# Decode attention with an MLP on one core: the output projection's weight moved behind the last V, read in contiguous rows and five pieces; the last V in wide form; o moved to the weight's layout by a matmul

## The chip, the cores and the metric

One core of a Trainium2 chip. The time is the device time of one execution in microseconds (us). Each kernel was executed several times; the text gives the median and the range. Profiles are single executions; their span, from the first to the last instruction, is 1.5 to 1.9 us shorter than the device time of the same execution. "Head n" counts from 0; the last head is 31. The granted clock is the share of its full clock that the profile records as given to TensorE. A transfer *lands* when its last completion signal arrives, and only then do the engines that wait for it go on. SBUF is the on-chip memory for operands, PSUM the one that TensorE writes its results to.

## The reference, cut to what matters

```python
# x: 1 x 640.  32 heads, 32768 cached keys, head size 128, all bf16.
xn = layernorm(x)
q = (xn @ wq) as 32 heads of 128
scores = q . k_cache[h] / sqrt(128);  p = softmax(scores);  o[h] = p @ v_cache[h]
out = x + concat(o) @ wo + (silu(xn @ w_gate) * (xn @ w_up)) @ w_down      # wo: 4096 x 640
```

K and V are 32 x 8.39 MB each and are read once: 537 of the 554 MB that the kernel moves. `wo`, the weight of the output projection, has 5.24 MB.

## The kernel before

Everything big passes through three slots of 64 KB per partition in SBUF (`ring`). SyncE issues all loads in one queue, in the order of `units`: wq, the MLP's weights, then K of head h and V of head h-1 in turn, then `wo`, then the last V in five pieces. A load waits until the slot's last reader is done.

```python
    TAIL = [128, 64, 32, 16, 16]          # the last V's pieces, in key blocks of 128 keys
    W = 512 // DH                         # 4
    ...
    units += [("wo",), ("v", H - 1)]
    ...
    # wo: partition = position within a head, so 32 rows of 1280 B for each partition
    e.dma_start(wo, A_wo.rearrange("(h d) n -> d h n", d=DH)).then_inc(s_wo, 16)
```

There are two forms of P·V. In the *wide* form (all heads but the last) four columns of P are the stationary operand and four V blocks stream past as 512 columns. The result lies in four partitions and must be copied out (`evac`), added up across partitions by eight small matmuls (`fold`) and written to the o column (`column`). In the *narrow* form (last head) one V block of 128 x 128 is the stationary operand and one column of P streams past; 256 such matmuls leave o as a finished column.

```python
    def pv_half(h, half):                                           # wide: 64 matmuls for a head
        for j in range(half * NJ // 2, (half + 1) * NJ // 2, W):
            mm = t.matmul(O, lhsT=P[:, h % PR, j:j + W], rhs=ring[:, s, j * DH:(j + W) * DH], ...)
    ...
    def pv_last():                                                  # narrow: 256 matmuls
        for i, n in enumerate(TAIL):
            t.wait_ge(s_tail[i], 16)
            for _ in range(n):
                mm = t.matmul(OL, lhsT=ring[:, s, j * DH:(j + 1) * DH], rhs=P[:, h % PR, j:j + 1], ...)
                j += 1
    ...
    def att(h):                                                     # projection: 5 matmuls for a head
        for c in range(NCD):
            mm = t.matmul(acc[:, c:c + 1], lhsT=wo_v[:, h, :, c], rhs=ocol[:, h:h + 1], ...)
        return mm
    ...
    # the end of TensorE's program (heads 2 to 31 are a loop of three heads a turn)
    fold(H - 2)
    t.wait_ge(s_wo, 16)
    for h in range(H - 1): att(h)         # 31 heads, 155 matmuls, while the last V lands
    total(H - 1)
    pv_last()
    t.wait_ge(s_ov, H)
    att(H - 1).then_inc(s_att, 1)         # 5 matmuls; then VectorE adds x, and the output is stored
```

## Time and profile before

| | before |
|---|---|
| time, median of 4 runs (range) | 1294.53 us (1294.24 to 1294.67) |
| span of the profiled run | 1292.7 us |
| bytes moved, mean rate over the span | 554 MB, 429 GB/s |
| last K lands / V of head 30 lands | 1234.5 / 1253.9 us |
| `wo` lands / last V's last piece lands | 1268.3 / 1287.8 us |
| granted TensorE clock, mean | 0.884 |

From the page of before: the span, and the busy share of the DMA engines in tenths and the GB/s that they moved, in 40 equal slices of the span.

```profile
span 1292.7 us, 9645 instructions
...
DMA  9999999999999999999999999999999999999997
GB/s 400 449 424 427 443 426 437 432 436 434 432 434 436 426 436 436 430 432 438 432 436 430 436 434 430 434 436 428 434 438 432 430 438 436 432 430 436 436 392 311
```

Read it as: the kernel is one stream of bytes, full from the start to the last slice. The chain of waits of before, its end (start in us, length, what):

```profile
1262.78 25.06 DMA ring<-in_A_v_cache_dram
...
1287.88 0.60 PE ps L279 x16
...
1288.51 0.23 DVE ocol L505
...
1288.79 0.37 PE ps L345 x5
...
1289.19 0.16 DVE outb L508
```

The last V piece lands at 1262.78 + 25.06 = 1287.84 us. Then come 16 narrow matmuls, a scaling on VectorE, 5 projection matmuls, the final addition, and the store. TensorE's part of the timeline of before (start, length, engine, line, operation, output<-inputs, shapes, count, and in brackets the idle time in front and what ended it):

```profile
1262.87 7.07 PE L266 MATMUL ps<-ring,P 128*4 128x512 bf16 x32
...
1273.40 6.33 PE L345 MATMUL ps<-ocol,ring 128*128 128x1 bf16 x155 [0.35 <-ACT ocol L391]
...
1280.02 1.76 PE L279 MATMUL ps<-P,ring 128*128 128x1 bf16 x61
1282.06 3.55 PE L279 MATMUL ps<-P,ring 128*128 128x1 bf16 x128 [0.27 <-issue]
1285.80 1.50 PE L279 MATMUL ps<-P,ring 128*128 128x1 bf16 x51 [0.19 <-issue]
1287.88 0.59 PE L279 MATMUL ps<-P,ring 128*128 128x1 bf16 x16 [0.59 <-DMA ring<-in_A_v_cache_dram]
1288.79 0.36 PE L345 MATMUL ps<-ocol,ring 128*128 128x1 bf16 x5 [0.32 <-DVE ocol L505]
```

L266 is wide P·V: 32 matmuls in 7.07 us, 221 ns each. L345 is the projection: 40 ns each. L279 is narrow P·V: 27 ns each, so 256 take about 7 us where the wide form takes 14.1 us. TensorE has hardly an idle moment between 1273.4 and 1287.3 us and then waits 0.59 us for the last piece. DMA and TensorE are nearly level at the end, and the 155 projection matmuls sit where the last V is still landing. Busy time by stretch, with the granted clock (PEclk), the DMA's busy share and GB/s:

```profile
core 0: us, PE busy (x) PEld busy (x) DVE busy (x) ACT busy (x) POOL busy (x), PEclk, DMA share, GB/s
...
1255.00:1261.00 6.00, 6.00 (x31) 2.49 (x28) 1.15 (x3) 0.00 (x0) 0.00 (x0) 1.00 1.07 363
...
1276.00:1280.00 4.00, 4.00 (x96) 4.00 (x95) 0.00 (x0) 0.00 (x0) 0.00 (x0) 0.50 0.98 414
...
1284.00:1288.00 4.00, 3.22 (x116) 3.08 (x114) 0.00 (x0) 0.00 (x0) 0.00 (x0) 0.50 0.20 77
```

Two things to see. In the stretch that carries `wo` (1255 to 1261) the DMA engines are fully busy but move 363 GB/s, not the 430 of the slices before. And from 1273.9 us on the granted clock is 0.50, although TensorE is busy all the time: with one-column matmuls.

### The profile page before, as it was taken

What the parts mean: (1) busy time and instruction counts of PE and PEld (TensorE: products, weight loads), DVE (VectorE), ACT (ScalarE), POOL (GpSimd) and SP (SyncE); (2) the same over time, 40 slices, a digit from 0 to 9 for tenths busy, and PEclk for the clock granted to TensorE, in tenths of its full rate; (3) what the DMA queues carried; (4) which work ended last, traced back from release to release, by engine and by line L of the source; (5) the groups of instructions that cost most, each with busy time, mean ns of one, the idle gap of its engine ahead of it and who ended that gap; (6) DMA issues with size and microseconds to landing.
All of it is one profiled execution on the core that took longest, in us unless ns stands there. A gap on an engine that the chain in (4) does not pass through costs nothing.

```text
span 1292.7 us, 9645 instructions
## 1 busy us (share of the span) xinstructions
PE 1040.2 (80%) x5147; PEld 264.2 (20%) x3227; DVE 669.9 (52%) x407; ACT 50.8 (4%) x139; POOL 1.1 (0%) x8
## 2 busy tenths in 40 slices
PE   4688879877779877779877779877778877779878
PEld 1301222111222111222111222111222111222116
DVE  0485544666444666444666444666444666444660
ACT  2000000000000000000000000000000000000000
POOL 0000000000000000000000000000000000000000
PEclk9588899888899888889888889888899888899887
DMA  9999999999999999999999999999999999999997
GB/s 400 449 424 427 443 426 437 432 436 434 432 434 436 426 436 436 430 432 438 432 436 430 436 434 430 434 436 428 434 438 432 430 438 436 432 430 436 436 392 311
DMA packets 14721, 554.20 MB, mean 429 GB/s; under 512 B 1329, under 2 KB 5490, under 8 KB 5746
## 3 DMA queue, kind: packets, MB, share of 16 engines
q1 hardware_dynamic: 14704, 554.00, 99.4%
q8 instruction: 9, 0.15, 0.0%
q14 instruction: 6, 0.05, 0.0%
q10 hardware_dynamic: 2, 0.00, 0.0%
HBM read 553.99 MB, written 0.00 MB: 429 GB/s over the span
## 4 chain that ended last, share of the span: by engine, by line
DMA 54%; PE 30%; DVE 13%; issue 2%; SPq 1%; DVEq 0%
DMA ring<-in_A_k_cache_dram 52%; PE ps L266 16%; DVE ring L479 13%; PE ps L227 12%; DMA ring<-in_A_v_cache_dram 2%; PE ps L254 1%; SPq L174 1%; PE ps L303 0%; PE ps L297 0%; SPq L183 0%; DVE sc L485 0%; PE ps L279 0%; SPq L185 0%; DVE pmax L491 0%; SPq L182 0%
## 5 line engine op out<-in xcount | busy, mean ns | idle before, releaser
L479 DVE TENSOR_TENSOR ring<-ring,qb 128x8192 bf16<-128x8192 bf16 x128 | 557.8, 4421 | 88.4 <-DMA ring<-in_A_k_cache_dram 88.4
L227 PE MATMUL ps<-ring,ident 128*128 128x512 bf16 x1920 | 498.7, 418 | 0.0
L266 PE MATMUL ps<-ring,P 128*4 128x512 bf16 x1984 | 438.3, 379 | 0.0
L254 PE MATMUL ps<-ring,ident 128*128 128x512 bf16 x128 | 56.1, 439 | 224.2 <-DVE ring L479 223.6
L266 PEld LDWEIGHTS ps<-ring,P 128*4 128x4 bf16 x1984 | 166.0, 85 | 245.4
L254 PEld LDWEIGHTS ps<-ring,ident 128*128 128x128 bf16 x128 | 12.6, 99 | 622.2 <-DVE ring L479 350.4
L499 DVE TENSOR_SCALAR negb<-ps 128x1 f32<-128x1 f32 x32 | 5.1, 158 | 215.5 <-PE ps L309 215.5
L485 DVE TENSOR_REDUCE sc<-ps 128x64 f32<-128x512 f32 x128 | 82.3, 686 | 63.0 <-PE ps L227 63.0
L494 DVE TENSOR_REDUCE m<-ps 1x1 f32<-1x128 f32 x32 | 8.9, 278 | 192.2 <-PE ps L303 192.2
L403 ACT ACTIVATE P<-sc,negb 128x256 bf16<-128x256 f32 x32 | 16.2, 508 | 1185.1 <-DVE negb L499 1185.1
L297 PEld LDWEIGHTS ps<-rsum,ones 128*128 128x128 f32 x64 | 12.3, 194 | 99.1 <-issue 98.3
L289 PE MATMUL ps<-identf,o 4*128 4x1 f32 x248 | 31.8, 245 | 0.9 <-ACT o L386 0.9
L289 PEld LDWEIGHTS ps<-identf,o 4*128 4x128 f32 x248 | 30.0, 187 | 0.9 <-ACT o L386 0.9
L386 ACT ACTIVATE o<-ps,rzb 4x512 f32<-4x512 f32 x31 | 21.0, 677 | 0.0
L219 PE MATMUL ps<-ring 128*128 128x512 bf16 x40 | 11.3, 455 | 11.0 <-DMA ring<-in_A_wq_dram 11.0
L449 DVE TENSOR_SCALAR sg<-sg 128x13 f32<-128x13 f32 (+1 forms) x2 | 0.2, 156 | 34.2 <-ACT sg L379 34.2
L491 DVE TENSOR_REDUCE pmax<-sc 128x1 f32<-128x256 f32 x32 | 13.4, 420 | 0.0
L303 PE MATMUL ps<-identf,pmax 128*1 128x128 f32 x64 | 12.2, 273 | 1.2 <-DVE pmax L491 1.2
L330 PE MATMUL ps<-xn,ring 128*128 128x1 bf16 (+1 forms) x140 | 8.8, 199 | 4.6 <-DMA ring<-in_B_w_down_dram 4.6
L309 PE MATMUL ps<-m,ones 1*128 1x1 f32 x64 | 12.1, 256 | 0.4 <-DVE m L494 0.4
L309 PEld LDWEIGHTS ps<-m,ones 1*128 1x128 f32 x64 | 9.4, 182 | 14.2 <-issue 13.5
L468 DVE RECIPROCAL rzb<-ps 128x1 f32<-128x1 f32 x32 | 5.1, 158 | 9.8 <-PE ps L297 9.8
(50 smaller groups left out, 88.8 us busy)
## 6 DMA issues: line engine op xcount, KB each, us to landing
ring<-in_A_wq_dram SPq DMA_DIRECT2D x1, 5120.0 KB, 15.2
ring<-in_A_wo_dram SPq DMA_DIRECT2D x1, 5120.0 KB, 37.0
ring<-in_A_v_cache_dram SPq DMA_DIRECT2D x1, 4096.0 KB, 22.3
ring<-in_B_w_gate_dram SPq DMA_DIRECT2D x1, 2160.0 KB, 19.9
ring<-in_B_w_up_dram SPq DMA_DIRECT2D x1, 2160.0 KB, 24.6
ring<-in_B_w_down_dram SPq DMA_DIRECT2D x1, 2080.0 KB, 28.5
ring<-in_A_v_cache_dram SPq DMA_DIRECT2D x1, 2048.0 KB, 21.6
ring<-in_A_v_cache_dram SPq DMA_DIRECT2D x1, 1024.0 KB, 23.6
```

What stands on the lines that cost most here:

```text
L174: e.dma_start(ring[:, s, j * DH:(j + n) * DH], kv_src(A_v_cache, u[1], j, n)).then_inc(s_tail[i], 16)
L227: return t.add_instruction(mybir.InstMatmult(start_tensor_calc=False, stop_tensor_calc=stop, tile_size=(128, 128), tile_position=(0, 0), l ...
L254: t.matmul(ob, lhsT=ident[:, :], rhs=src, start=True, stop=False)
L266: mm = t.matmul(O, lhsT=P[:, h % PR, j:j + W], rhs=ring[:, s, j * DH:(j + W) * DH], start=(j == 0), stop=(j + W == NJ))
L289: mm = t.matmul(fold_ps, lhsT=o4[:, m * DH:(m + 1) * DH], rhs=identf[0:W, m:m + 1], start=(m == 0), stop=(m == W - 1))
L297: t.matmul(misc[:, 129:130], lhsT=ones[:, :], rhs=rsum[:, h % SR:h % SR + 1], start=True, stop=True).then_inc(s_z, 1)
L309: t.matmul(misc[:, 128:129], lhsT=ones[0:1, :], rhs=m1[0:1, h % SR:h % SR + 1], start=True, stop=True).then_inc(s_b, 1)
L386: a.activation(out=o4[:, :], in_=O, func=ACTF.Copy, scale=rzb[0:W, h % SR:h % SR + 1]).then_inc(s_o4, 1)
L403: a.activation(out=P[:, h % PR, :], in_=sc[:, :], func=ACTF.Exp, bias=negb[:, h % SR:h % SR + 1], scale=c_scale, accum_out=rsum[:, h % SR: ...
L479: v.tensor_tensor(out=kh, in0=kh, in1=q[:, None, :].to_broadcast([128, HF, DH]), op=ALU.mult).then_inc(s_mul, 1)
L485: v.tensor_reduce(out=sc[:, i * HF:(i + 1) * HF], in_=bank[i].rearrange("p (j e) -> p j e", e=G), axis=AX.X, op=ALU.add).then_inc(s_red, 1)
L491: v.tensor_reduce(out=pmax[:, h % SR:h % SR + 1], in_=sc[:, :], axis=AX.X, op=ALU.max).then_inc(s_max, 1)
```

## The change

The intent: read `wo` in long rows, which need a layout where partition p holds rows 32p to 32p+31; put it last, in pieces, so that the end of the stream is followed by only 10 projection matmuls; bring o into the same layout by one matmul. The last V takes the wide form, as the other heads have it. The diff, cut:

```diff
-    TAIL = [128, 64, 32, 16, 16]
+    TAIL = [128, 64, 32, 32]
+    RB = DH // 32; OC = H * DH // 128; WTAIL = [16, 8, 4, 2, 2]
-    units += [("wo",), ("v", H - 1)]
+    units += [("v", H - 1), ("wo",)]
...
-   e.dma_start(wo, A_wo.rearrange("(h d) n -> d h n", d=DH)).then_inc(s_wo, 16)
+   wo_src = A_wo.rearrange("(p j) n -> p (j n)", j=OC)
+   for i, n in enumerate(WTAIL):
+       e.dma_start(wo[:, j * D:(j + n) * D], wo_src[:, j * D:(j + n) * D]).then_inc(s_wo[i], 16)
+       j += n
...  pv_last:
+   t.wait_ge(s_o4, h)
-   for _ in range(n):
-       mm = t.matmul(OL, lhsT=ring[:, s, j * DH:(j + 1) * DH], rhs=P[:, h % PR, j:j + 1], ...)
-       j += 1
+   for _ in range(n // W):
+       mm = t.matmul(O, lhsT=P[:, h % PR, j:j + W], rhs=ring[:, s, j * DH:(j + W) * DH], ...)
+       j += W
...  the end of TensorE's program:
    fold(H - 2)
-   (wait for wo; att(0) to att(30))
    total(H - 1)
    pv_last()
-   t.wait_ge(s_ov, H); att(H - 1)
+   fold(H - 1)
+   t.wait_ge(s_ob, 1)
+   t.matmul(op, lhsT=oblk[:, :, :], rhs=fold32[:, :], start=True, stop=True)     # moves o
+   t.wait_ge(s_ot, 1)
+   for i, n in enumerate(WTAIL):
+       t.wait_ge(s_wo[i], 16)
+       (n x 5 projection matmuls: lhsT=wo_v[:, j, :, c], rhs=ot[:, j:j + 1])
...  ScalarE: evac(31), column(31), copy op -> ot;  VectorE: oblk = o columns x block pattern
```

Constants for the movement are made by GpSimd at the start.

More of the change, by code (lines that the diff above doesn't have):

```diff
@@ L46, in bass_parallel_sum__gqa_block_cached__swiglu_ffn__decode_kernel @@
     SR = 3
-    TAIL = [128, 64, 32, 16, 16]
+    TAIL = [128, 64, 32, 32]
+    RB = DH // 32
+    OC = H * DH // 128
+    WTAIL = [16, 8, 4, 2, 2]
     W = 512 // DH
-    assert sum(TAIL) == NJ and NHF == 4 and (H - H0) % PER == 0 and PER % SLOTS == 0
+    assert sum(TAIL) == NJ and all(n % W == 0 for n in TAIL) and NHF == 4 and (H - H0) % PER == 0 and PER % SLOTS == 0
     assert PER % PR == 0 and PER % SR == 0
+    assert OC == 32 and H * RB == 128 and sum(WTAIL) == OC
     c_scale = float(DH) ** -0.5
@@ L87, in bass_parallel_sum__gqa_block_cached__swiglu_ffn__decode_kernel @@
         ocol = sbt("ocol", [128, H], BF16)
+        oblk = sbt("oblk", [128, H, RB], BF16)
+        blk = sbt("blk", [128, RB], BF16)
+        fold32 = sbt("fold32", [128, OC], BF16)
+        ot = sbt("ot", [128, OC], BF16)
         hcol = sbt("hcol", [128, FB], BF16)
@@ L103, in bass_parallel_sum__gqa_block_cached__swiglu_ffn__decode_kernel @@
         s_slot = [sem(f"slot{i}") for i in range(SLOTS)]
-        s_x, s_wq, s_wo, s_out = sem("x"), sem("wq"), sem("wo"), sem("o")
+        s_x, s_wq, s_out = sem("x"), sem("wq"), sem("o")
+        s_wo = [sem(f"wo{i}") for i in range(len(WTAIL))]
         s_ffn = sem("ffn")
@@ L118, in bass_parallel_sum__gqa_block_cached__swiglu_ffn__decode_kernel @@
         s_att, s_fin = sem("att"), sem("fin")
+        s_ob, s_op, s_ot = sem("o_blocks"), sem("o_ps"), sem("o_rows")
         block = es.enter_context(nc.Block())
@@ L142, in hidden @@
             return w[:, c, FM * 128:F]
-        wo = flat[:, WO_S * CE:WO_S * CE + H * D].rearrange("p (h n) -> p h n", h=H)
-        wo_v = wo.rearrange("p h (m c) -> p h m c", c=NCD)
-        assert H * D <= CE
+        wo = flat[:, WO_S * CE:WO_S * CE + OC * D]
+        wo_v = wo.rearrange("p (j m c) -> p j m c", j=OC, c=NCD)
+        assert OC * D <= CE
         def kv_src(cache, h, j0, n):
@@ L152, in bass_parallel_sum__gqa_block_cached__swiglu_ffn__decode_kernel @@
             O = ps8[0:W, 4, :]
-            OL = ps8[:, 5, 0:1]
+            op = ps8[:, 5, 0:OC]
             acc = ps8[:, 6, 0:NCD]
@@ L187, in sp @@
                     else:
-                        e.dma_start(wo, A_wo.rearrange("(h d) n -> d h n", d=DH)).then_inc(s_wo, 16)
+                        wo_src = A_wo.rearrange("(p j) n -> p (j n)", j=OC)
+                        j = 0
+                        for i, n in enumerate(WTAIL):
+                            e.dma_start(wo[:, j * D:(j + n) * D], wo_src[:, j * D:(j + n) * D]).then_inc(s_wo[i], 16)
+                            j += n
                 e.wait_ge(s_fin, 1)
@@ L194, in pool, with done @@
             def pool(g):
-                for n, t in enumerate((ident, identf)):
-                    g.memset(t[:, :], 0.0).then_inc(s_const, 1)
-                    g.wait_ge(s_const, 2 * n + 1)
-                    g.affine_select(out=t[:, :], in_=t[:, :], compare_op=ALU.not_equal, fill=1.0, base=0,
-                                    pattern=[[-1, 128]], channel_multiplier=1).then_inc(s_const, 1)
+                n = [0]
+                def done(ins):
+                    ins.then_inc(s_const, 1)
+                    n[0] += 1
+                    g.wait_ge(s_const, n[0])
+                for t in (ident, identf):
+                    done(g.memset(t[:, :], 0.0))
+                    done(g.affine_select(out=t[:, :], in_=t[:, :], compare_op=ALU.not_equal, fill=1.0, base=0,
+                                         pattern=[[-1, 128]], channel_multiplier=1))
+                done(g.memset(blk[:, :], 0.0))
+                for a in range(RB):
+                    done(g.tensor_copy(out=fold32[a * 32:(a + 1) * 32, :],
+                                       in_=ident[a * 32:(a + 1) * 32, a * 32:a * 32 + OC]))
+                for a in range(RB):
+                    done(g.memset(blk[a * 32:(a + 1) * 32, a:a + 1], 1.0))
+                assert n[0] == 5 + 2 * RB
             @block.tensor
@@ L277, in pv_last @@
                         t.wait_ge(s_tail[i], 16)
-                        for _ in range(n):
-                            mm = t.matmul(OL, lhsT=ring[:, s, j * DH:(j + 1) * DH], rhs=P[:, h % PR, j:j + 1],
-                                          start=(j == 0), stop=(j == NJ - 1))
-                            j += 1
+                        for _ in range(n // W):
+                            mm = t.matmul(O, lhsT=P[:, h % PR, j:j + W], rhs=ring[:, s, j * DH:(j + W) * DH],
+                                          start=(j == 0), stop=(j + W == NJ))
+                            j += W
                     mm.then_inc(s_pv, 1)
@@ L341, in pe @@
                 mm.then_inc(s_fpd, 1)
-                def att(h):
-                    for c in range(NCD):
-                        mm = t.matmul(acc[:, c:c + 1], lhsT=wo_v[:, h, :, c], rhs=ocol[:, h:h + 1],
-                                      start=(h == 0 and c == 0), stop=(h == H - 1), skip_group_check=True)
-                    return mm
                 t.wait_ge(s_fx, 1)
@@ L357, in pe @@
                 fold(H - 2)
-                t.wait_ge(s_wo, 16)
-                t.wait_ge(s_ov, H - 1)
-                for h in range(H - 1):
-                    att(h)
                 total(H - 1)
                 pv_last()
-                t.wait_ge(s_ov, H)
-                att(H - 1).then_inc(s_att, 1)
+                fold(H - 1)
+                t.wait_ge(s_const, 5 + 2 * RB)
+                t.wait_ge(s_ob, 1)
+                t.matmul(op, lhsT=oblk[:, :, :], rhs=fold32[:, :], start=True, stop=True).then_inc(s_op, 1)
+                t.wait_ge(s_ot, 1)
+                j = 0
+                for i, n in enumerate(WTAIL):
+                    t.wait_ge(s_wo[i], 16)
+                    for _ in range(n):
+                        for c in range(NCD):
+                            mm = t.matmul(acc[:, c:c + 1], lhsT=wo_v[:, j, :, c], rhs=ot[:, j:j + 1],
+                                          start=(j == 0 and c == 0), stop=(j == OC - 1), skip_group_check=True)
+                        j += 1
+                mm.then_inc(s_att, 1)
             @block.scalar
@@ L408, in act @@
                 column(H - 2)
+                evac(H - 1)
+                column(H - 1)
+                a.wait_ge(s_op, 1)
+                a.activation(out=ot[:, :], in_=op, func=ACTF.Copy).then_inc(s_ot, 1)
             @block.vector
@@ L501, in dve @@
                 rz(H - 1)
-                h = H - 1
-                v.wait_ge(s_pv, H)
-                v.wait_ge(s_rz, H)
-                v.tensor_scalar(out=ocol[:, h:h + 1], in0=OL, scalar1=rzb[:, h % SR:h % SR + 1],
-                                scalar2=None, op0=ALU.mult).then_inc(s_ov, 1)
+                v.wait_ge(s_const, 5 + 2 * RB)
+                v.wait_ge(s_ov, H)
+                v.tensor_tensor(out=oblk[:, :, :], in0=ocol[:, :, None].to_broadcast([128, H, RB]),
+                                in1=blk[:, None, :].to_broadcast([128, H, RB]), op=ALU.mult).then_inc(s_ob, 1)
                 v.wait_ge(s_att, 1)
```

## The prediction

> **What bounds it now.** The page shows DMA busy in every slice, 429 GB/s over the span, and a chain of waits that is 54% DMA. That stream stays. The change touches the last 40 us, where the timeline and the table of windows say more than shares:
> - V of head 30 lands at 1253.8 us. From 1255.7 TensorE is busy nearly all the time: P·V of head 30 until 1269.9, its fold until 1273.05, 155 projection matmuls from 1273.4 (6.3 us, 40 ns each), 256 narrow P·V matmuls of the last head from 1279.8 (27 ns each, 7.1 us without waits), ending 1288.5. The last V piece lands at 1287.85: DMA is the limit by about half a microsecond only.
> - The span ends at 1292.7, 3.5 us after the last projection matmul.
>
> **What the change does.**
> 1. Weight rows of 1280 B become rows of 2.5 to 20 KB. In the windows that carry the weight (1254 to 1262) the DMA moves 363 GB/s at full busy share, against about 430 with V or K. Estimate: its 5.24 MB take 14.4 us now, 12.4 after. The Trainium skill, "DMA: Bandwidth & Descriptors", "Why small descriptors are slow", gives a fixed cost per packet; the trace agrees in direction. So the last byte lands about 2 us earlier, near 1285.8.
> 2. The last V in wide form: 64 matmuls of 512 columns. The loop's same form takes 7.07 us for 32 at full clock, so 14.1 us against 7.1. It cannot start before 1273.3: P of the last head exists at 1271.2 and fold(30) ends at 1273.05. V, moved ahead of the weight, is all there by about 1275, so this is TensorE time, not waiting.
> 3. Clock: TensorE does little between 1269.9 and 1273.3. The windows show the granted clock falling to 0.5 at 1273.9 in just this place; in earlier heads it comes back after a full busy window. The Trainium skill, "TensorE: Matmul & The Clock Gate", Part 1, has free-running windows of 3.4 us, and the clock record changes on that grid. So 3.4 to 6 us of the wide stage run at half clock: +1.7 to 3 us, my mean 1.9.
> 4. Then a new serial chain: evacuation 0.73, fold 1.08, column 0.2, block product about 0.3, movement matmul about 0.4, copy and hops about 0.4: 3.1 us.
> 5. Only then all 160 projection matmuls: 6.4 us, of which 155 stood earlier before and filled the time in which V was landing.
>
> **On the critical path.** TensorE becomes the limit by a wide margin: 1273.35 + 14.1 + 1.9 + 3.1 + 6.4 + 3.5 = 1302.4 us of span against 1292.7. The 2 us that DMA gains are not seen; the weight is complete before its matmuls begin. So +9.7 us: **1304.1 us**, 8 in 10 between 1301 and 1307. Chances: faster over 2% 0.01, within 2% 0.97, slower over 2% 0.02.
>
> **What would show it.** Everything up to 1270 unchanged; last weight piece landing near 1286; wide matmuls from about 1273.3 to 1289, part at half clock; no DMA wait in front of the projection matmuls, which run from about 1292.4 to 1298.8; the end of the chain of waits made of TensorE, with DMA idle for the last 13 us but for the output.
>
> **What would make it wrong.** If the clock does not fall (about 1302), or stays low over the wide stage (up to 1309). If projection matmuls run faster at full clock (up to 3 us less). If pieces came late enough for DMA to bound the end after all: about 1292 to 1294.

## The result, and the profile after

| | before | after |
|---|---|---|
| time, median (range), first 4 runs of each | 1294.53 (1294.24 to 1294.67) | 1304.58 (1302.02 to 1305.76) |
| ratio of the fast runs | | 1.0074, 95% interval 1.006 to 1.0089 |
| time, second set: 9 runs before, 5 runs after | 1294.21 (1293.92 to 1294.51) | 1303.80 (1303.37 to 1305.03) |
| ratio, second set | | 1.0076, interval 1.0062 to 1.009 |
| span of the profiled run | 1292.7 | 1302.0 |
| V of head 30 / last V / last of `wo` lands | 1253.9 / 1287.8 / 1268.3 | 1254.0 / 1273.6 / 1285.9 |
| spread of the runs, highest less lowest, first set | 0.43 | 3.74 |

The result is slower by 0.75% clear of noise.

From the page of after, the lines that answer to those of before:

```profile
span 1302.0 us, 9298 instructions
...
DMA  9999999999999999999999999999999999999994
GB/s 397 446 425 442 423 435 429 437 433 431 437 433 433 435 435 429 441 425 435 433 433 437 433 433 435 435 431 437 427 433 435 431 437 433 433 437 433 435 414 172
```

The last slice falls from 311 to 172 GB/s: the stream ends earlier, and the kernel later. The chain of waits of after, its end:

```profile
1272.17 1.05 PE ps L317 x8
1273.22 0.31 PE ps L325 x2
1273.54 15.61 PE ps L307 x64
...
1289.16 0.69 ACT o L417
...
1289.89 1.06 PE ps L317 x8
...
1290.98 0.18 ACT ocol L422
...
1291.26 0.30 DVE oblk L539
...
1291.69 0.19 PE ps L386
...
1291.91 0.21 ACT ot L443
...
1292.16 6.57 PE ps L393 x160
...
1298.76 0.16 DVE outb L542
```

No DMA stands in it after the last K, up to the final store. From 1273.5 us: wide P·V (L307), copy out, fold (L317), column, block product, movement matmul (L386), copy, and the 160 projection matmuls (L393). Busy time by stretch:

```profile
core 0: us, PE busy (x) PEld busy (x) DVE busy (x) ACT busy (x) POOL busy (x), PEclk, DMA share, GB/s
...
1272.00:1276.00 4.00, 3.83 (x17) 2.08 (x18) 0.17 (x1) 0.30 (x2) 0.00 (x0) 0.73 0.96 411
1276.00:1280.00 4.00, 4.00 (x17) 1.49 (x16) 0.00 (x0) 0.00 (x0) 0.00 (x0) 0.84 0.97 408
1280.00:1284.00 4.00, 4.00 (x21) 1.53 (x18) 0.00 (x0) 0.00 (x0) 0.00 (x0) 1.00 0.66 264
1284.00:1288.00 4.00, 4.00 (x20) 1.61 (x19) 0.00 (x0) 0.00 (x0) 0.00 (x0) 1.00 0.02 9
```

The clock drops to half at 1273.84 us and returns at 1277.25 us by the clock record, so 3.4 us of the wide stage ran at half speed. The stage took 15.66 us in place of 14.1. The DMA share is 0.02 from 1284 to 1288 us and 0.04 or less later, while the core computes for 13 us more.

Step by step, from the wide stage's start to the end of the span, in us:

| term | predicted | profiled run |
|---|---|---|
| wide stage starts | 1273.35 | 1273.46 |
| 64 wide matmuls at full clock + half clock | 14.1 + 1.9 | 15.66 in all |
| from their end to the first projection matmul | 3.1 | 3.0 |
| 160 projection matmuls | 6.4 | 6.57 |
| to the end of the span | 3.5 | 3.3 |
| last byte of `wo` lands | 1285.8 | 1285.9 |
| span | 1302.4 | 1302.0 |

### The profile page after: what moved, and what is told of

It is laid out like the page before. It is cut to its first block, busy times and chain, and to the rows that moved or that the text cites. A ratio compares the mean times of both kernels' runs of the same rounds, so it can differ in the third digit from the quotient of the medians.

```text
span 1302.0 us, 9298 instructions
## 1 busy us (share of the span) xinstructions
PE 1045.6 (80%) x4964; PEld 263.7 (20%) x3044; DVE 669.9 (51%) x407; ACT 51.9 (4%) x142; POOL 2.5 (0%) x17
## 4 chain that ended last, share of the span: by engine, by line
DMA 52%; PE 34%; DVE 12%; issue 2%; SPq 0%; ACT 0%; DVEq 0%
DMA ring<-in_A_k_cache_dram 52%; PE ps L293 17%; PE ps L254 13%; DVE ring L514 12%; PE ps L281 1%; PE ps L307 1%; PE ps L393 1%; PE ps L331 0%; PE ps L317 0%; PE ps L325 0%; ACT o L417 0%; SPq L193 0%; DVE sc L520 0%; PE ps L337 0%; SPq L195 0%
## 5 line engine op out<-in xcount | busy, mean ns | idle before, releaser
L293 PE MATMUL ps<-ring,P 128*4 128x512 bf16 x1984 | 438.3, 379 | 0.0
L317 PE MATMUL ps<-identf,o 4*128 4x1 f32 x256 | 32.9, 245 | 1.6 <-ACT o L417 1.6
L317 PEld LDWEIGHTS ps<-identf,o 4*128 4x128 f32 x256 | 31.0, 187 | 2.2 <-ACT o L417 2.2
L417 ACT ACTIVATE o<-ps,rzb 4x512 f32<-4x512 f32 x32 | 21.7, 678 | 15.7 <-PE ps L307 15.7
L307 PE MATMUL ps<-ring,P 128*4 128x512 bf16 x64 | 15.7, 411 | 0.0
```

Of the source, the lines that this page charges most:

```text
L317: mm = t.matmul(fold_ps, lhsT=o4[:, m * DH:(m + 1) * DH], rhs=identf[0:W, m:m + 1], start=(m == 0), stop=(m == W - 1))
L417: a.activation(out=o4[:, :], in_=O, func=ACTF.Copy, scale=rzb[0:W, h % SR:h % SR + 1]).then_inc(s_o4, 1)
```

## The experiments

Eleven kernels ran, all gave the right result. Each was timed in 5 rounds beside the kernel before on the same chip, so before has 9 runs in each of the three sets: medians 1294.21, 1294.27 and 1294.15 us. Line numbers differ between kernels by a few.

The theory, called A: after the last V the kernel is bound by TensorE's serial work, and the wide form is what makes it so. The rivals: the moved projection is the cost (B), the spread and the long wide stage are not the clock (C), the pieces matter. A further question, instruction fetch (D), came up on the way.

### Narrow last V in the changed kernel

```diff
 (after)  pv_last:
-   for _ in range(n // W): matmul(O, lhsT=P[.., j:j + W], rhs=ring[.. W blocks])
+   for _ in range(n): matmul(OL, lhsT=ring[.. block j], rhs=P[.., j:j + 1])
-   fold(H - 1);  evac(H - 1);  column(H - 1)
+   VectorE: ocol[:, 31] = OL * rz(31)
```

> The changed kernel with one part undone: the last V in narrow form again (256 matmuls of one column, output scaled straight into the o column; no evacuation, no fold). Weight still last, contiguous, five pieces, movement matmul kept. Theory A (the wide form is the cost, by TensorE time): narrow stage 1273.5 to 1280.4 us, block product, movement and copy until about 1281.7, 160 projection matmuls until 1288.2 with little or no wait for the weight pieces, span 1291.7, time about 1293.5 us, 1.0 us below the kernel before. Rival B (the order is the cost: 155 projection matmuls no longer fill the time in which V lands): about 6 us above the kernel before, 1299 to 1301 us, whatever the form.

Measured: 1295.21 us (1294.79 to 1295.46), ratio 1.0007 (0.9994 to 1.0021). TensorE's part of its timeline:

```profile
1273.56 5.92 PE L307 MATMUL ps<-P,ring 128*128 128x1 bf16 x217
1281.53 1.20 PE L307 MATMUL ps<-P,ring 128*128 128x1 bf16 x39 [2.04 <-issue]
...
1284.00 6.56 PE L392 MATMUL ps<-ot,ring 128*128 128x1 bf16 x160 [0.29 <-ACT ot L440]
```

Undoing the wide form alone takes back 8.6 of the 9.6 us (1303.80 to 1295.21). B expected 1299 to 1301 and falls: with the weight still last and all 160 projection matmuls behind the last V, the kernel is within 1.0 us of before. The 1.7 us over my expectation of 1293.5 come from a stop of 2.04 us after 217 of 256 matmuls, put down to "issue", that is, to nothing which the profile shows. It is taken up below. By the two profiles the 8.6 us are about these terms: 14.0 us of wide matmuls against 7.1 us of narrow ones, 1.7 us of half clock, 1.8 us more from the end of the stage to the first projection matmul (3.04 against 1.27 us, for evacuation and fold), less the 2.0 us of the stop.

### Wide last V in the kernel before

```diff
 (before)  pv_last: wide form as in the change;  then
+   fold(H - 1, into another bank);  evac(H - 1);  column(H - 1)
-   VectorE: ocol[:, 31] = OL * rz(31)
```

> The kernel before with one part of the change alone: the last V in wide form (evacuation, fold, column for head 31 as for the others), order and layout of the weight as before. Theory A: 155 projection matmuls until 1279.6 us as before, then 64 wide matmuls, the first 4 us of them at half clock, until about 1296, then evacuation, fold and column 2.1 us, 5 matmuls, span about 1302, time about 1304 us (9.5 us above before). Rival B: the wide matmuls hide behind the landing V, so only the last piece's 4 matmuls and the 2 us of evacuation show: 1295 to 1297 us.

Measured: 1304.06 us (1303.1 to 1304.24), ratio 1.0074 (1.006 to 1.0088). TensorE's timeline:

```profile
1273.70 6.33 PE L346 MATMUL ps<-ocol,ring 128*128 128x1 bf16 x155 [0.35 <-ACT ocol L393]
...
1280.39 16.25 PE L280 MATMUL ps<-ring,P 128*4 128x512 bf16 x64
...
1298.73 0.36 PE L346 MATMUL ps<-ocol,ring 128*128 128x1 bf16 x5 [0.27 <-ACT ocol L393]
```

The wide form alone costs 9.9 us here, without any of the other parts. The matmuls do not hide behind the landing V: the last piece is there at 1288.2 us, and the stage runs until 1296.6. It took 16.25 us, with the clock at half until 1285.0 us. With this run the four combinations are complete:

| last V | `wo` first, 1280 B rows | `wo` last, long rows, pieces, movement |
|---|---|---|
| narrow | 1294.2 | 1295.2 |
| wide | 1304.1 | 1303.8 |

The form decides, in either column; order and layout together move the time by 1 us or less.

### Keeping the clock up

```diff
 (after)
+   4 wide matmuls on old data, result thrown away
    fold(H - 2)
    total(H - 1)
+   4 more
    pv_last()
```

> The changed kernel with 8 wide matmuls on old data (result thrown away) put around the fold of head 30, where TensorE idles. Theory A says that the granted clock falls because that window has little wide work, and that this costs 1.7 to 3 us in the wide stage, varying with the phase of the clock's windows from run to run: here the clock should stay at 1.0, the wide stage take 14.1 us and start 0.9 us later, time about 1303.5 us with a spread under 1 us. Rival C (the spread over runs and the long wide stage have another cause, such as reads of V in competition with the landing weight): stage still 15.7 us, time about 1305.5 us, spread 2 to 4 us.

Measured: 1302.75 us (1302.65 to 1303.11), with 8 matmuls more than the changed kernel. Two rows of its busy time by stretch, and the wide stage in its timeline:

```profile
1272.00:1276.00 4.00, 4.00 (x24) 2.22 (x23) 0.17 (x1) 0.60 (x2) 0.00 (x0) 1.00 0.99 421
1276.00:1280.00 4.00, 4.00 (x20) 1.57 (x19) 0.00 (x0) 0.00 (x0) 0.00 (x0) 1.00 0.97 408
```

```profile
1274.66 13.98 PE L307 MATMUL ps<-ring,P 128*4 128x512 bf16 x64
```

The clock stays at 1.00 where it was 0.73 and 0.84. The stage starts 1.2 us later and takes 13.98 in place of 15.66 us. The spread over five runs is 0.46 us. So C falls: the fall of the clock is what lengthens the wide stage. The weight still landed during the stage here and did not lengthen it. That the fall comes at different moments in different runs, and so makes the spread of after, is a reading that fits and is not shown: the clock of the wide stage was seen in the profiled runs only, and the mean clock that each run lists (0.879 to 0.891 for the changed kernel) does not settle it. The nine times of the changed kernel lie within 0.4 us of 1302.0, 1303.7 or 1305.4 us, in steps of the 1.7 us that one such stretch at half clock costs.

### The changed kernel again

No edit; five more runs, with the profile.

> The changed kernel once more, for the spread over runs: both theories expect 1302 to 1306 us; theory A expects a wide stage of 14.1 us plus half of the time at half clock within it, whatever the profiled run shows.

Measured: 1303.80 us (1303.37 to 1305.03). The profiled run has the same wide stage, 15.66 us, of which 3.4 us at half clock by the clock record (1273.87 to 1277.29): 14.0 + 3.4 / 2 = 15.7. The range of the two sets together is 1302.02 to 1305.76 us.

### `wo` in one transfer, wide and narrow

```diff
-    WTAIL = [16, 8, 4, 2, 2]
+    WTAIL = [32]
```

> The changed kernel with the weight in one transfer in place of five. Theory A (TensorE time after the last V is the limit, the weight is there long before): no change, 1303 to 1305 us, with the transfer landed near 1286 us and the first projection matmul near 1292 us. Rival (the pieces are what makes the late weight bearable): 3 us or more slower than the changed kernel.

Measured on the changed kernel: 1303.59 us (1301.99 to 1303.74). The transfer landed at 1285.7 us; the first projection matmul started at 1292.2. Five pieces gain nothing there, because the weight is not what is waited for.

> The changed kernel with the narrow last V and the weight in one transfer. Here the projection was ready to start at 1284.0 us and the last byte came at 1285.8 us, so one transfer makes all 160 matmuls wait for it: start near 1286 us, about 2 us later than with five pieces, time about 1297.2 us against 1295.2 us. If pieces cost something of their own, the difference is smaller.

Measured with the narrow V: 1297.14 us (1297.05 to 1297.26), 1.9 us over five pieces.

```profile
1285.70 6.53 PE L392 MATMUL ps<-ot,ring 128*128 128x1 bf16 x160 [2.83 <-DMA ring<-in_A_wo_dram]
```

The projection was ready at about 1283.1 us (the copy of o had ended) and waited until the transfer landed at 1285.6. The stop after 217 narrow matmuls is here too, at 1.57 us. The pieces are worth something only after the wide form is gone.

### `wo` first in the queue, but contiguous

```diff
 (narrow V)
-    units += [("v", H - 1), ("wo",)];   TAIL = [128, 64, 32, 32]
+    units += [("wo",), ("v", H - 1)];   TAIL = [128, 64, 32, 16, 16]
```

> The changed kernel with the narrow last V and the weight ahead of it in the queue, as in the kernel before, but contiguous. Theory A: the transfer of the weight takes about 12.4 us in place of 14.4 us, the last V byte lands near 1285.8 us (1287.8 us before), but the o layout needs every head, so all 160 projection matmuls (6.5 us) stand after the last V: span about 1297.4 us, time about 1299 us. If the contiguous read itself gained nothing, the last V would land near 1287.8 us and the time be about 1301 us.

Measured: 1299.42 us (1299.14 to 1299.71). `wo` landed at 1266.2 us, 12.4 us after V of head 30 (1268.3 in before, 14.4 us after it), and the last V piece at 1285.8 (1287.8 in before). So the contiguous layout saves 2.0 us of DMA time. But in the new layout a column of o holds a part of every head, so no projection matmul can start before the last head is done: the first was at 1287.7 us, and 160 of them stood behind the last byte. In this layout the 2.0 us can be of use only with the order "weight last".

### The stop in the narrow stage: instruction fetch

In the narrow run the profile (its packed trace, packet by packet) has a packet of 16384 B in the queue that it calls "instruction", starting at 1279.0 us and taking 1.07 us; TensorE stopped from 1279.5 to 1281.5. The Trainium skill, "Runtime: NRT & Kernel Launch", "Instruction fetch mechanics", says that instructions are fetched in 16 KiB blocks of 256 (called pages below), the next while the current one runs. One narrow matmul is a weight load and a matmul, so 256 instructions are 128 pairs. If that is the cause, the stop belongs to a place in the instruction stream and must move when instructions are put in front.

```diff
 (narrow V)  at the start, where TensorE waits for data
+   for _ in range(90): matmul(unused column, lhsT=ident, rhs=ident[:, 0:1])
```

> The changed kernel with the narrow last V, and 90 matmuls of no use at the start of the kernel, where TensorE waits for data. In the run with the narrow last V, TensorE stood still for 2.04 us after 217 of 256 narrow matmuls, while a 16 KB packet of an instruction queue went over the DMA engines. Theory D (instruction fetch: the stream of short unrolled matmuls reaches a page of 256 instructions, or 128 load and matmul pairs, before it is there): the stop moves by 90 pairs to earlier places, after 127 and 255 matmuls, where the next one falls into the wait for VectorE and ScalarE; it shows less or not at all, time 1293.3 to 1294.3 us. Rival E (the stop belongs to the data, the landing of V or the weight): it stays after 217 matmuls, at 2 us, time 1295.2 us.

Measured: 1296.89 us (1296.59 to 1297.3). TensorE's timeline:

```profile
1273.30 3.47 PE L309 MATMUL ps<-P,ring 128*128 128x1 bf16 x127
1278.79 3.57 PE L309 MATMUL ps<-P,ring 128*128 128x1 bf16 x128 [2.02 <-issue]
1283.63 0.19 PE L309 MATMUL ps<-P,ring 128*128 128x1 bf16 x1 [1.27 <-issue]
```

The stops are after 127 and after 255 matmuls, as D says: 217 - 90 = 127, and one page further. E falls: the data came at the same times as in the run before (the last V at 1273.5 us in both). My time was wrong: I had expected the first stop to shrink in its new place, and it stayed at 2.02 us, with a second of 1.27 us behind it.

The kernel before has such stops as well, short ones: in its timeline above the idle times of 0.27 and 0.19 us put down to "issue" stand after 61 and after 189 narrow matmuls, 128 apart, and packets of 16384 B started at 1279.59 and 1283.46 us.

One estimate covers most of the stops. Taking a page to be entered 128 pairs before its end, at 25 to 27 ns a pair, the next page's first instruction ran 5.6 us after that entry in the narrow run (entered at about 1275.9 us, resumed at 1281.53) and 5.5 and 4.8 us in this one. A page of narrow pairs is used up in 3.2 to 3.4 us. It does not cover the second stop of before: that page was entered at 1282.06 us and the next one ran at 1285.80, 3.7 us later. What all eleven stops in the traces of this document share is the time from the start of the packet until TensorE goes on: 2.3 to 2.6 us. What varies is how long after the estimated entry the packet starts: 1.4 us at that stop, about 2.5 to 3.7 us at the others. Why it starts late is not shown, and that the fetch is asked for at the entry is inferred, not seen. The wide form never shows a stop: 128 wide pairs would last 28 us.

### Versions meant to beat both

```diff
 (narrow V)
-   fold(H - 2);  total(H - 1);  pv_last()
+   total(H - 1);  the first 128 narrow matmuls;  fold(H - 2);  the other 128
-   VectorE: ocol[:, 31] = OL * rz;  oblk = all columns x blk
+   VectorE, early: oblk of heads 0 to 30;  at the end: oblk[:, 31] = OL * rz * blk in one operation
```

> A version meant to beat both kernels: the changed kernel with the narrow last V, its first 128 matmuls put ahead of the fold of head 30 (TensorE idles there for 0.86 us), and the o block of the last head made in one VectorE operation straight from PSUM. By theory A and D: narrow stage from 1271.4 us, 7 us of matmuls, 1 us of fold and one stop of 1 to 2 us for an instruction page; block, movement and copy 0.9 us; projection from about 1282 to 1289 us; time about 1293.5 us (1292.5 to 1294), 0.7 us below the kernel before. If the stop does not depend on the instruction's place, or the earlier start runs into another wait, 1294.5 us or more.

Measured: 1293.19 us (1292.82 to 1293.31) against 1294.15 (1293.91 to 1294.39) before; ratio 0.9992, interval 0.9978 to 1.0005. TensorE's timeline:

```profile
1271.45 3.37 PE L309 MATMUL ps<-P,ring 128*128 128x1 bf16 x128
1274.76 1.86 PE L319 MATMUL ps<-identf,o 4*128 4x1 f32 x8
1276.55 2.53 PE L309 MATMUL ps<-P,ring 128*128 128x1 bf16 x89
1279.47 1.20 PE L309 MATMUL ps<-P,ring 128*128 128x1 bf16 x39 [0.40 <-issue]
...
1281.55 6.56 PE L393 MATMUL ps<-ot,ring 128*128 128x1 bf16 x160 [0.29 <-ACT ot L441]
```

Every run of it lies below every run of before, by 0.96 us in the median, but the interval does not exclude equal. It is 10.6 us under the changed kernel (1303.80). The stop after 217 matmuls has shrunk to 0.40 us: the fold in the middle, 1.9 us long, gives the fetch more time.

Then the last three heads were written out, so that the stream would run straight on and be fetched ahead:

```diff
-   with t.Fori(0, (H - H0) // PER) as i: ...
+   with t.Fori(0, (H - H0) // PER - 1) as i: ...
+   for h in range(H - PER, H): head(h)
```

> The same, with the last three heads taken out of TensorE's loop and written out, so that the instruction stream goes straight on through the slow wide matmuls of the last heads and pages can be fetched ahead. Theory D: the first page boundary in the narrow stage has been fetched in time, a second one 128 pairs later may still stop TensorE for up to 2 us; time 1291.8 us without a stop, 1293.8 us with one. If the stop is not instruction fetch, the time is that of the run before it in this set. Written-out heads could also stop at their own pages, before 1270 us; they have slack only where TensorE waits for VectorE.

Measured: 1296.28 us (1296.02 to 1296.45), a miss. Lines of TensorE's timeline:

```profile
1277.63 0.37 PE L319 MATMUL ps<-identf,o 4*128 4x1 f32 x2 [1.76 <-issue]
...
1283.83 0.19 PE L309 MATMUL ps<-P,ring 128*128 128x1 bf16 x2 [2.38 <-issue]
```

Both page ends fell into the narrow stage, after 134 and 262 pairs counted from its start with the fold, and both stopped it. Writing the heads out did not bring the pages sooner: the packets of the two started at 1275.0 and 1281.3 us, not in the 30 us before. By the estimate above the pages were entered at about 1271.5 and 1277.6 us and the next ones ran 6.1 and 6.2 us later. So the loop in front of the narrow stage is not what makes the packets late. I had taken more than one page to be fetched ahead; nothing here shows that.

> The same with 64 idle load and matmul pairs at the start, which move every page boundary by half a page: theory D expects any stop in the narrow stage or the projection to move by 64 pairs to earlier places; time 1291.8 to 1293.8 us.

Measured: 1293.88 us (1293.44 to 1294.53).

```profile
1279.25 1.90 PE L311 MATMUL ps<-P,ring 128*128 128x1 bf16 x66 [0.84 <-issue]
...
1285.33 4.12 PE L397 MATMUL ps<-ot,ring 128*128 128x1 bf16 x100 [0.74 <-issue]
```

The stops came after 198 pairs (262 - 64; 0.84 us) and 60 matmuls into the projection (0.74 us), half a page earlier than in the run before, as D says. The same program, moved by 64 pairs, is 2.4 us faster. The reading that fits: a stop costs less when the pairs of the page before it take longer, as those of the fold and of the projection do (40 ns a pair in the projection).

## Why the prediction was right

The time was 1304.58 us, predicted 1304.1 with 1301 to 1307; the second set's median was 1303.80. Point by point:

1. *Long rows save about 2 us of DMA.* Shown: 12.3 us from the last V's landing to the last byte of `wo` in after, 14.4 us for the same bytes before, and 12.4 us with the order kept. The Trainium skill, "DMA: Bandwidth & Descriptors", "Why small descriptors are slow", gives a fixed cost per packet; the change of rate from 363 GB/s agrees in direction. How much of the 2 us is row length and how much another part of the layout, no run takes apart. As predicted, nothing of it reached the time.
2. *The wide form costs twice the TensorE time, and it is not waiting.* Shown by both single exchanges: 8.6 us taken back in the changed kernel, 9.9 us added in the kernel before. The doubled matmul time itself is 7 us of it (14.0 against 7.1); the rest is the clock of point 3 and the evacuation and fold of point 4, which go with the form.
3. *The clock falls for want of work before the wide stage.* Shown: it fell at 1273.84 us, 0.4 us after the stage had begun, and for 3.4 us, which is 1.7 us of cost; with the gap before it filled it does not fall. The spread over runs shrinks too; that the clock made it fits and is not shown. The Trainium skill, "TensorE: Matmul & The Clock Gate", Part 1, describes a free-running window of about 3.4 us; the clock record's step of 3.4 us agrees. I had the mean a little high (1.9).
4. *The new serial chain of about 3.1 us.* It was 3.0.
5. *All 160 projection matmuls come last.* True as a description, and their 6.57 us are in the chain. But the prediction gave this step as if it were a cost of its own, beside the wide form. The runs show otherwise: with the narrow form, order, layout, pieces and movement together cost 1.0 us, with 2.0 us of stop inside (the kernel before has 0.5 us of its own). Moving the projection behind the last V is nearly free, because the narrow P·V takes the place it left and the weight lands meanwhile.

What the prediction did not foresee was the instruction fetch. It did not touch the changed kernel's time, but it set what a repair gained: the narrow form alone came to 1295.21 us where its terms gave 1293.5, and the version with the fold in the middle, whose stop is 0.40 us, to 1293.19 us.

## What to carry to other kernels

Before moving a transfer to the end of a stream, add up what the compute engine still has to do after its own last input: here DMA and TensorE were level within half a microsecond, so a form that added 7 us of matmuls to one TensorE stage, with what goes with it, made the kernel 8.6 us slower. Exchange the parts of a composite change one by one in both directions: four cells put the 9.6 us on the one part that looked like a detail. And where a stage is made of very short instructions, look for idle time put down to "issue" at even distances in the instruction stream, and fill the place with something slow.

## What the Trainium skill lacked or had wrong

- "Runtime: NRT & Kernel Launch", "Instruction fetch mechanics", calls the cost of crossing a 16 KiB boundary mostly hidden. In streams of load and matmul pairs at 25 to 40 ns a pair, eleven crossings cost between 0.19 and 2.38 us, five of them over 1.5 us (1.57, 1.76, 2.02, 2.04 and 2.38). The page gives no time for a fetch; here TensorE went on 2.3 to 2.6 us after the packet had started, of which the packet itself took 1.02 to 1.11 us, and by the estimate above 3.7 to 6.2 us after it had entered the page before.
- "TensorE: Matmul & The Clock Gate", Part 1, speaks of busy and idle windows without saying what counts as busy (Part 4 sets only transposes apart). Here the granted clock stayed at 0.50 from 1273.9 us to the end in before, while one-column matmuls kept TensorE busy for 4.00 of 4.00 us (1276 to 1280); and it fell at 1273.84 us in after, when the 3.4 us before had held 0.9 us of idle time, small matmuls for most of the rest, and 0.4 us of wide ones. With eight wide matmuls added around that place it stayed at 1.00.
- The same page, Part 2, "LDWEIGHTS" and the section on Fast Weight Load, gives P / 1.2 ns for a load of P columns and a measured speed-up of about 2. That makes about 53 ns for 128 columns, an estimate from the page. Here a pair of a 128-column bf16 load and a one-column matmul took 26.7 ns at half clock (the narrow run) and 25 ns at full clock (the first 110 pairs of the version meant to beat both). The first is what 32 cycles make at the page's 1.2 GHz, the figure that its table has as theory for fp8; the second agrees with the page's floor of about 25 ns between matmuls. Whether Fast Weight Load was on, the traces do not say.
- That page has no time for weights read with a stride, and the note on strides in "SBUF — State Buffer" has none for weight loads either. The projection's weights are every fifth bf16 element, and its pairs took 40 ns at either clock, where the narrow pairs of contiguous weights took 25 to 27 ns; that the stride is the cause was not tested.
